# An attention-plus-MLP block on one core: a start for 512 tokens at a time, feature-major queries with block-ones sums, key normalisers moved to v, Mish in one instruction, both output products in one accumulation

## The chip, the core and the metric

The kernel runs on one core of one Trainium2 chip. A core has a tensor engine (PE), a vector engine (DVE), a scalar engine (ACT), GpSimd (POOL) and DMA queues. The metric is the device time of one execution in microseconds (us). Matmul results land in PSUM, which a kernel divides into banks; the program writes a bank again only when the engine that reads it is done. The granted clock is the share of its full speed that the profile records for PE. A profile's span, from its first to its last instruction, is about 1.7 us shorter than the measured time of the same execution.

## The reference, cut to what matters

There are S = 2048 tokens of width D = 512, 32 heads of width 16, and a hidden layer of F = 1792. All tensors are bf16.

```python
xn = layernorm(x)
# branch A: linear attention whose feature map is two softmaxes over 16 features
q, k, v = split_heads(xn @ wqkv)
pq, pk  = q @ w_phi, k @ w_phi                            # per head, 16x16
phi_q = concat(softmax(pq), softmax(-pq))
phi_k = concat(softmax(pk), softmax(-pk))
kv, z = sum_s phi_k[s] v[s]^T, sum_s phi_k[s]
o     = (phi_q @ kv) / (phi_q @ z + 1e-6)
A     = merge_heads(o) @ wo
# branch B: MLP with Mish
h = xn @ w1 + b1
B = (h * tanh(softplus(h))) @ w2
return x + A + B
```

`kv` and `z` sum over all tokens, so no token's attention output can begin before the last group of keys is in. Everything else can be done for one group of 512 tokens after another.

## The kernel before

The head projections are folded into the weights once (`wqp`, `wkp`). Then there is a loop over four groups of 512 tokens, and a closing phase for the attention output. The parts that the argument touches are these:

```python
# start: loads on two queues, statistics of ALL tokens before the loop
nc.scalar.dma_start(wqk[:], ...)            # 1 MB; scalar issues the loads of w1, w2 and the bias too
...
nc.scalar.dma_start(b1b[:], b1_v[:, :])     # 1792 biases, one element per descriptor
...
st[0] = stage_front(0)
finish_ln_stats()                           # loads the other 12 token tiles, bn_stats, one Sqrt

# stage_front: k and q token-major (tokens on partitions), exponentials of both
e1 = exp(ppkq); e2 = exp(-ppkq)             # 128 x 1024: plane 0 is k, plane 1 is q

# stage_phi: sums of 16 neighbours, normalise k twice and q once, all on the vector engine
nc.vector.reduce_sum(ss1[:], e1...);  nc.vector.reduce_sum(ss2[:], e2...)
...                                         # reciprocals, then e1k*=r1, e2k*=rk2, e1q*=ratio
# stage_kq: 32 tensor transposes and 8 vector copies turn q feature-major
# stage_h: uu = exp(h + b)                  (14 tiles of 128x512)
# stage_lt: Mish in three passes over 128 x 7168
nc.scalar.activation(th[:], uu[:], ACT.Ln, bias=1.0)      # softplus
nc.scalar.activation(uu[:], uu[:], ACT.Ln)                # h again
nc.scalar.activation(th[:], th[:], ACT.Tanh)
# stage_mb: act = lnu * th on vector (14 tiles), poB = act @ w2, copied to xb_all

for g in range(NG):
    uu = stage_h(st[g])
    if g > 0:
        stage_mb(st[g - 1], lt[g - 1])      # the PREVIOUS group's output product fills the passes
    lt[g] = stage_lt(uu)
    stage_phi(st[g]); stage_kq(st[g])
    if g + 1 < NG:
        st[g + 1] = stage_front(g + 1)
... kvm = kvacc * mask;  stage_mb(last)
# closing phase, per 512 tokens: attention products, normalise o, transpose,
# poA = ident @ x + oT @ wo, y = poA + xb_all
```

One property of the closing dependence helps later: the softmax of q needs no normaliser of its own. A common factor of both softmax planes cancels in `num / den`, so only the ratio of the two sums matters. The kernel before uses that (`ratio`).

The softmax here doesn't subtract the row's maximum and nothing guards it: scores larger than these inputs give would overflow.

Of the kernel before, what the change touches and what calls it, by code (L numbers as in the profile page):

```python
# [8 lines left out]
BF16 = mybir.dt.bfloat16  # L9
FP32 = mybir.dt.float32  # L10
# [7 lines left out]
def kernel(  # L18
# [12 lines left out]
    nc = tc.nc  # L31
# [6 lines left out]
    FT = F // P  # L38

    x2 = A_x.flatten_outer_dims()  # L40
    x_g = x2.rearrange("(g t p) d -> g p t d", t=TPG, p=P)
    o2 = out.flatten_outer_dims()
    out_g = o2.rearrange("(g t p) d -> g p t d", t=TPG, p=P)
# [5 lines left out]
    b1_v = B_b1.rearrange("(f p) -> p f", p=P)  # L49
# [5 lines left out]
    ident = consts.tile([P, P], BF16, name="ident")  # L55
    make_identity(nc, ident[:])

    U16f = consts.tile([8, P], FP32, name="U16f")
    nc.gpsimd.memset(U16f[:], 1.0)
    nc.gpsimd.affine_select(  # L60
        out=U16f[:],
        in_=U16f[:],
        pattern=[[1, P]],
        compare_op=ALU.is_ge,
        fill=0.0,
        base=0,
        channel_multiplier=-16,
    )
    nc.gpsimd.affine_select(
        out=U16f[:],  # L70
        in_=U16f[:],
        pattern=[[-1, P]],
        compare_op=ALU.is_ge,
        fill=0.0,
        base=15,
        channel_multiplier=16,
    )
    eps_t = consts.tile([P, 1], FP32, name="eps_t")
    nc.gpsimd.memset(eps_t[:], 1e-5)

    prep_w = tc.alloc_tile_pool(name="prep_w", bufs=1)
    xs_v = x2.rearrange("(g t p) d -> p (g t) d", t=TPG, p=P)
    x_stats0 = prep_w.tile([P, TPG, D], BF16, name="x_stats0")
    nc.sync.dma_start(x_stats0[:], xs_v[:, 0:TPG, :])
    wqk = prep_w.tile([P, KT, 2 * D], BF16, name="wqk")
    nc.scalar.dma_start(wqk[:], wqkv_v[:, :, 0 : 2 * D])
# [4 lines left out]
    nc.sync.dma_start(wv[:], wqkv_v[:, :, 2 * D : 3 * D])  # L91
    w1_sb = wts.tile([P, KT, F], BF16, name="w1_sb")
    nc.scalar.dma_start(w1_sb[:], w1_v[:, :, :])
    wo_sb = wts.tile([P, KT, D], BF16, name="wo_sb")
    nc.sync.dma_start(wo_sb[:], wo_v[:, :, :])
    w2_sb = wts.tile([P, FT, D], BF16, name="w2_sb")
    nc.scalar.dma_start(w2_sb[:], w2_v[:, :, :])
    b1b = wts.tile([P, FT], BF16, name="b1b")
    with nc.allow_non_contiguous_dma(reason="tiny bias load"):
        nc.scalar.dma_start(b1b[:], b1_v[:, :])  # L100
    b1f = wts.tile([P, FT], FP32, name="b1f")
    nc.vector.tensor_copy(b1f[:], b1b[:])

    phiqT_all = persist.tile([P, 8, S], BF16, name="phiqT_all")
    kvacc = persist.tile([P, 8, 136], FP32, name="kvacc")
    kvm = persist.tile([P, 8, 136], BF16, name="kvm")
    xb_all = persist.tile([P, NT, D], BF16, name="xb_all")
    mv = persist.tile([P, NT, nc.vector.BN_AGGR_DIM], FP32, name="mv")
    rstd = persist.tile([P, NT], FP32, name="rstd")

    stats0 = prep_w.tile([P, TPG, nc.vector.BN_STATS_DIM], FP32, name="stats0")
    for tt in range(TPG):
        nc.vector.bn_stats(stats0[:, tt, :], x_stats0[:, tt, :])
    for tt in range(TPG):
        nc.vector.bn_aggr(mv[:, tt, :], stats0[:, tt, :])
    nc.scalar.activation(rstd[:, 0:TPG], mv[:, 0:TPG, 1], ACT.Sqrt, bias=eps_t[:])
    nc.vector.reciprocal(rstd[:, 0:TPG], rstd[:, 0:TPG])

    def finish_ln_stats():
        statpool = tc.alloc_tile_pool(name="statpool", bufs=1)  # L120
        x_stats = statpool.tile([P, NT - TPG, D], BF16, name="x_stats")
        nc.sync.dma_start(x_stats[:], xs_v[:, TPG:NT, :])
        stats = statpool.tile([P, NT, nc.vector.BN_STATS_DIM], FP32, name="stats")
        for tt in range(TPG, NT):
            nc.vector.bn_stats(stats[:, tt, :], x_stats[:, tt - TPG, :])  # L125
        for tt in range(TPG, NT):
            nc.vector.bn_aggr(mv[:, tt, :], stats[:, tt, :])
        nc.scalar.activation(rstd[:, TPG:NT], mv[:, TPG:NT, 1], ACT.Sqrt, bias=eps_t[:])
        nc.vector.reciprocal(rstd[:, TPG:NT], rstd[:, TPG:NT])
        statpool.release()  # L130

    KVmask = consts.tile([P, 136], FP32, name="KVmask")
    B16b = consts.tile([P, P], BF16, name="B16b")
    Wbd = prep_w.tile([P, 4, P], BF16, name="Wbd")
# [3 lines left out]
    with ExitStack() as pctx:  # L138
        ps_prep = pctx.enter_context(
            tc.tile_pool(name="ps_prep", bufs=2, space=bass.MemoryType.PSUM)  # L140
        )
        ps_fold = pctx.enter_context(
            tc.tile_pool(name="ps_fold", bufs=4, space=bass.MemoryType.PSUM)
        )
        tmp = pctx.enter_context(tc.tile_pool(name="prep_tmp", bufs=2))

        pB = ps_prep.tile([P, P], FP32, name="pB", tag="prep")
        nc.tensor.matmul(pB[:], lhsT=U16f[:], rhs=U16f[:], start=True, stop=True)
        nc.vector.tensor_copy(B16b[:], pB[:])
        nc.vector.tensor_copy(KVmask[:, 0:P], pB[:])  # L150
        nc.vector.tensor_copy(KVmask[:, P : P + 8], pB[:, 0:P:16])

        nc.vector.tensor_tensor(
            out=Wbd[:].rearrange("p j (i e) -> p j i e", e=DH),
            in0=B16b[:, None, :]
            .rearrange("p o (i e) -> p o i e", e=DH)
            .to_broadcast([P, 4, 8, DH]),
            in1=Wsrc[:, :, None, :].to_broadcast([P, 4, 8, DH]),
            op=ALU.mult,
        )  # L160

        for mi, base_col in ((0, 0), (1, D)):
            pfs = [
                ps_fold.tile([P, D], FP32, name=f"pfold{mi}_{kt}", tag="fold")
                for kt in range(KT)
            ]
            for j in range(4):
                ptr = ps_prep.tile([P, D], BF16, name="ptrw", tag="prep")
                for kt in range(KT):
                    nc.tensor.transpose(  # L170
                        ptr[:, kt * P : (kt + 1) * P],
                        wqk[:, kt, base_col + j * P : base_col + (j + 1) * P],
                        ident[:],
                    )
                wT = tmp.tile([P, D], BF16, name="wT")
                nc.scalar.copy(wT[:], ptr[:])
                for kt in range(KT):
                    nc.tensor.matmul(
                        pfs[kt][:, j * P : (j + 1) * P],
                        lhsT=wT[:, kt * P : (kt + 1) * P],  # L180
                        rhs=Wbd[:, j, :],
                        start=True,
                        stop=True,
                    )
            dst = wqp if mi == 0 else wkp
            for kt in range(KT):
                nc.vector.tensor_copy(dst[:, kt, :], pfs[kt][:])
    prep_w.release()

    with ExitStack() as p1:  # L190
        xpool = p1.enter_context(tc.tile_pool(name="pa_x", bufs=1))
        xnpool = p1.enter_context(tc.tile_pool(name="pa_xn", bufs=1))
        xnTpool = p1.enter_context(tc.tile_pool(name="pa_xnT", bufs=2))
        spool = p1.enter_context(tc.tile_pool(name="pa_small", bufs=4))
        epool = p1.enter_context(tc.tile_pool(name="pa_e", bufs=4))
        vpool = p1.enter_context(tc.tile_pool(name="pa_v", bufs=2))
        mpool = p1.enter_context(tc.tile_pool(name="pa_mish", bufs=1))
        apool = p1.enter_context(tc.tile_pool(name="pa_act", bufs=14))
        ps_tr = p1.enter_context(tc.tile_pool(name="ps_tr", bufs=1, space=bass.MemoryType.PSUM))
        ps_kq = p1.enter_context(tc.tile_pool(name="ps_kq", bufs=1, space=bass.MemoryType.PSUM))  # L200
        ps_mm = p1.enter_context(tc.tile_pool(name="ps_mm", bufs=2, space=bass.MemoryType.PSUM))
        ps_kv = p1.enter_context(tc.tile_pool(name="ps_kv", bufs=1, space=bass.MemoryType.PSUM))
        ps_oB = p1.enter_context(tc.tile_pool(name="ps_oB", bufs=2, space=bass.MemoryType.PSUM))

        def stage_front(g):
            xg = xpool.tile([P, TPG, D], BF16, name="xg")
            nc.sync.dma_start(xg[:], x_g[g])
            xn = xnpool.tile([P, TPG, D], BF16, name="xn")
            for t in range(TPG):
                tt = g * TPG + t  # L210
                nc.vector.tensor_scalar(
                    out=xn[:, t, :],
                    in0=xg[:, t, :],
# [193 lines left out]
        for g in range(NG):  # L407
            uu = stage_h(st[g])
            if g > 0:
                stage_mb(st[g - 1], lt[g - 1])  # L410
# [120 lines left out]
```

## Time and profile before

| | us |
|---|---|
| time, median of 3 runs | 282.98 (282.32 to 284.24) |
| span of the profiled run | 281.6 |
| PE busy | 215.3 (76%), so idle 66.3 |
| vector busy | 198.0 (70%) |
| scalar busy | 167.0 (59%) |
| first dense projection matmul (a single one runs at 43.58) | 45.06 |

The first lines are from the page of the kernel before. They give busy time by engine (busy us, share of the span, number of instructions), then the span in 40 slices of 7 us, with each digit the busy tenths of a slice.

```profile
PE 215.3 (76%) x1277; PEld 108.9 (39%) x1298; DVE 198.0 (70%) x504; ACT 167.0 (59%) x136; POOL 2.1 (1%) x14
...
PE   1122238898783699986999996899997589889973
...
ACT  0040110777999587899787899868799900320330
```

No engine is full. PE has six slices of 1 to 3 at the left, dips to between 3 and 6 in the middle (about one per group), and a soft right end. The next view gives busy us per stage: the stretch and its length, then busy us and instruction count of each engine, the granted clock, and the DMA share and rate. The stretches are the start, the four groups, the last hidden output, and the attention output.

```profile
0.00:45.00 45.00, 11.70 (x80) 8.44 (x82) 19.05 (x53) 5.95 (x11) 1.64 (x12) 1.00 0.62 197
45.00:94.00 49.00, 38.10 (x218) 18.64 (x219) 35.71 (x73) 39.93 (x30) 0.20 (x1) 0.97 0.07 23
...
133.00:178.00 45.00, 41.48 (x239) 20.39 (x241) 36.76 (x78) 39.42 (x28) 0.00 (x0) 1.00 0.00 1
...
240.00:282.00 42.00, 32.33 (x240) 16.80 (x243) 28.57 (x128) 8.72 (x16) 0.00 (x0) 0.97 0.23 76
```

The start costs PE 33 us of idleness, and the last stretch 10. What PE waited for is named by the table of waits of the kernel before (waiting instruction, its releaser, us in all, times, longest):

```profile
PE pfold_0_185 L178 <- DVE wqp L187: 10.7, 1, 10.7
PE pfold_0_133 L178 <- ACT wT L176: 8.3, 2, 8.0
PE ptr L325 <- DVE phiqT_all L330: 8.2, 26, 0.7
PE poB L392 <- DVE act L384: 7.1, 2, 6.3
PE ptrw L170 <- DMA wqk<-in_A_wqkv_dram: 5.4, 1, 5.4
```

Three of these (10.7, 8.3 and 5.4) belong to the start. The scalar engine's copies (`wT`) come late because it issues loads first; the bias load alone took 8.14 us to issue, until 16.5. The chain of waits shows the rest. It holds a load of 21.78 us, then ten statistics instructions; the small weight copy that PE needed (`wqp`) stands behind them in the vector engine's order.

```profile
2.38 21.78 DMA x_stats<-in_A_x_dram
24.18 6.03 DVE stats L125 x10
...
32.94 2.34 DVE wqp L187 x4
```

The 8.2 us in 26 pieces is an alternation of transposes and vector copies. The 7.1 us is the Mish: the timeline of the scalar engine in group 0 (start, duration, instruction) shows a table load, two passes, another table load and a third pass, in which PE at last runs dry.

```profile
71.89 1.28 ACT L373 ACT_TABLE_LOAD   x1
73.19 6.18 ACT L373 ACTIVATE th<-uu 128x7168 bf16<-128x7168 bf16 x1
79.40 6.18 ACT L374 ACTIVATE uu<-uu 128x7168 bf16<-128x7168 bf16 x1
85.59 1.28 ACT L375 ACT_TABLE_LOAD   x1
86.89 6.18 ACT L375 ACTIVATE th<-th 128x7168 bf16<-128x7168 bf16 x1
```

### The profile page before, as it was taken

Reading aid. Unit: us, or ns where it says so; the run is one execution under the profiler, and the core shown is the slowest. Engines: PE = TensorE matmul, PEld = TensorE weight load, DVE = VectorE, ACT = ScalarE, POOL = GpSimd, SP = SyncE. Lnnn points to the kernel's source line nnn. Section 1 sums busy time; section 2 is a strip of 40 time slices with the busy share of each in tenths; the row PEclk is TensorE's granted clock in tenths of the full one; section 3 lists DMA queues with packets and bytes.
Section 4 is the critical chain, followed back from the end, with each engine's and each line's share of the span. In section 5 each row is a group of like instructions: output and inputs, shape, how many; then the busy total and the mean of one; then the engine's idle time right before and its main releaser. Section 6 shows DMA issues by size and latency. Waiting matters only on the chain.

```text
span 281.6 us, 3341 instructions
## 1 busy us (share of the span) xinstructions
PE 215.3 (76%) x1277; PEld 108.9 (39%) x1298; DVE 198.0 (70%) x504; ACT 167.0 (59%) x136; POOL 2.1 (1%) x14
## 2 busy tenths in 40 slices
PE   1122238898783699986999996899997589889973
PEld 0122214343541244445444445444444434444531
DVE  0405955999761799736899947699965783788762
ACT  0040110777999587899787899868799900320330
POOL 2000000000000000000000000000000000000000
PEclk9999999999999599999999999999999989999998
DMA  7996022200002000000000000000000300043022
GB/s 221 369 356 175 0 74 78 74 0 0 2 0 74 0 1 2 1 0 2 0 0 0 2 0 0 2 0 1 2 0 0 129 22 0 0 152 121 30 74 74
DMA packets 14687, 14.38 MB, mean 51 GB/s; under 512 B 2640, under 2 KB 13648, under 8 KB 14672
## 3 DMA queue, kind: packets, MB, share of 16 engines
q1 hardware_dynamic: 7360, 7.34, 8.0%
q10 hardware_dynamic: 7312, 6.84, 7.6%
q8 instruction: 10, 0.16, 0.2%
q14 instruction: 5, 0.04, 0.1%
HBM read 12.08 MB, written 2.10 MB: 50 GB/s over the span
## 4 chain that ended last, share of the span: by engine, by line
PE 52%; ACT 18%; DVE 13%; DMA 8%; issue 7%; SPq 1%; ACTq 0%; DVEq 0%
PE poB L392 13%; PE pmm L359 13%; DMA x_stats<-in_A_x_dram 8%; PE ppkq L249 5%; PE ppkq L257 5%; PE poA L490 5%; ACT th L373 4%; ACT th L375 4%; PE pmm L237 4%; DVE stats L125 3%; DVE o_t L458 2%; DVE phiqT_all L330 2%; PE ptr L325 2%; PE ptr L223 2%; DVE yg L497 1%
## 5 line engine op out<-in xcount | busy, mean ns | idle before, releaser
L392 PE MATMUL poB<-w_sb,act 128*128 128x512 bf16 x218 | 51.8, 387 | 7.3 <-DVE act L384 7.1
L359 PE MATMUL pmm<-xnT,w_sb 128*128 128x512 bf16 x219 | 52.1, 378 | 1.1 <-ACT uu L366 0.8
L366 ACT ACTIVATE uu<-pmm,b1f 128x512 bf16<-128x512 f32 x56 | 37.2, 691 | 11.8 <-PE pmm L359 7.6
L392 PEld LDWEIGHTS <-act 128*128 128x128 bf16 x224 | 22.2, 99 | 34.9 <-DVE act L384 9.3
L359 PEld LDWEIGHTS <-w_sb 128*128 128x128 bf16 x224 | 21.8, 97 | 28.9 <-issue 4.7
L400 DVE CAST xb_all<-poB 128x512 bf16<-128x512 f32 x16 | 11.1, 691 | 20.8 <-PE poB L392 20.8
L384 DVE TENSOR_TENSOR act<-uu,th 128x512 bf16<-128x512 bf16 x56 | 19.6, 416 | 7.9 <-ACT th L375 7.9
L374 ACT ACTIVATE uu<-uu 128x7168 bf16<-128x7168 bf16 x4 | 24.7, 6177 | 0.1
L373 ACT ACTIVATE th<-uu 128x7168 bf16<-128x7168 bf16 x4 | 24.7, 6177 | 0.0
L375 ACT ACTIVATE th<-th 128x7168 bf16<-128x7168 bf16 x4 | 24.7, 6177 | 0.0
L237 PE MATMUL pmm<-wv,xnT 128*128 128x512 bf16 x64 | 20.1, 395 | 0.2
L249 PE MATMUL ppkq<-wkp,xnT 128*128 128x512 bf16 x58 | 17.9, 400 | 1.2 <-ACT e_349 L267 0.5
L330 DVE COPY phiqT_all<-ptr 128x512 bf16<-128x512 bf16 x32 | 13.6, 424 | 7.1 <-PE ptr L325 7.0
L257 PE MATMUL ppkq<-wqp,xnT 128*128 128x512 bf16 x64 | 17.3, 394 | 0.0
L497 DVE TENSOR_TENSOR yg<-poA,xb_all 128x512 bf16<-128x512 f32 x16 | 10.7, 689 | 8.9 <-PE poA L490 8.7
L449 PE MATMUL pnd<-kvm,phiqT_all 128*128 128x136 bf16 x128 | 14.1, 228 | 3.6 <-DVE kvm L416 1.9
L125 DVE BATCH_NORM_STATS2 stats<-x_stats 128x6 f32<-128x512 bf16 x12 | 7.3, 676 | 13.6 <-DMA x_stats<-in_A_x_dram 13.6
L458 DVE TENSOR_TENSOR o_t<-pnd,rdt 128x128 bf16<-128x128 f32 x64 | 15.9, 286 | 0.1
L490 PE MATMUL poA<-wo_sb,oT 128*128 128x512 bf16 x60 | 15.7, 379 | 0.1
L223 PE MATMUL ptr<-ident,xn 128*128 128x128 bf16 x64 | 7.6, 238 | 7.5 <-issue 4.0
L228 DVE COPY xnT<-ptr 128x512 bf16<-128x512 bf16 x16 | 6.8, 425 | 8.5 <-PE ptr L223 8.5
L449 PEld LDWEIGHTS <-phiqT_all 128*128 128x128 bf16 x128 | 8.3, 98 | 10.9 <-DVE o_t L458 6.5
(386 smaller groups left out, 352.3 us busy)
## 6 DMA issues: line engine op xcount, KB each, us to landing
w_sb<-in_B_w_dram ACTq DMA_DIRECT2D x2, 1792.0 KB, 18.8
xg<-in_A_x_dram SPq DMA_DIRECT2D x4, 512.0 KB, 3.4
out_dram<-yg SPq DMA_DIRECT2D x4, 512.0 KB, 3.2
x_stats<-in_A_x_dram SPq DMA_DIRECT2D x1, 1536.0 KB, 21.8
wqk<-in_A_wqkv_dram ACTq DMA_DIRECT2D x1, 1024.0 KB, 7.5
x_stats_78<-in_A_x_dram SPq DMA_DIRECT2D x1, 512.0 KB, 6.1
wv<-in_A_wqkv_dram SPq DMA_DIRECT2D x1, 512.0 KB, 8.2
wo_sb<-in_A_wo_dram SPq DMA_DIRECT2D x1, 512.0 KB, 12.2
```

The source lines that it names most:

```text
L237: nc.tensor.matmul(pv[:], lhsT=xnT[:, kt, tok0 : tok0 + P], rhs=wv[:, kt, :], start=(kt == 0), stop=(kt == KT - 1),)
L249: nc.tensor.matmul(ppkq[:, 0, :], lhsT=xnT[:, kt, tok0 : tok0 + P], rhs=wkp[:, kt, :], start=(kt == 0), stop=(kt == KT - 1),)
L257: nc.tensor.matmul(ppkq[:, 1, :], lhsT=xnT[:, kt, tok0 : tok0 + P], rhs=wqp[:, kt, :], start=(kt == 0), stop=(kt == KT - 1),)
L359: nc.tensor.matmul(ph[:], lhsT=w1_sb[:, kt, f * P : (f + 1) * P], rhs=xnT[:, kt, :], start=(kt == 0), stop=(kt == KT - 1),)
L366: nc.scalar.activation(uu[:, f, :], ph[:], ACT.Exp, bias=b1f[:, f : f + 1])
L373: nc.scalar.activation(th[:], uu[:], ACT.Ln, bias=1.0)
L374: nc.scalar.activation(uu[:], uu[:], ACT.Ln)
L375: nc.scalar.activation(th[:], th[:], ACT.Tanh)
L392: nc.tensor.matmul(poB[:], lhsT=acts[f][:, t * P : (t + 1) * P], rhs=w2_sb[:, f, :], start=(f == 0), stop=(f == FT - 1),)
L449: nc.tensor.matmul(pnd[:], lhsT=phiqT_all[:, s, tok0 : tok0 + P], rhs=kvm[:, s, :], start=(pl == 0), stop=(pl == 1),)
L458: nc.vector.tensor_tensor(out=o_t[:, j * P : (j + 1) * P].rearrange("p (h e) -> p h e", e=16), in0=pnd[:, 0:128].rearrange("p (h e) -> p h ...
L490: nc.tensor.matmul(poA[:], lhsT=oT[:, j, t * P : (t + 1) * P], rhs=wo_sb[:, j, :], start=False, stop=(j == 3),)
```

## The change

The intent is to take work from the vector and scalar engines, so that PE runs without stalls. The core of the diff, with cuts (`...`), and comments added for the reader:

```diff
 # start: 512 tokens first, statistics per group, weights on the sync queue, bias as rows
-    nc.scalar.dma_start(wqk[:], wqkv_v[:, :, 0 : 2 * D])
+    for t in range(TPG):
+        nc.sync.dma_start(xgs[0][:, t, :], x_t[t])
+    nc.scalar.dma_start(wk_raw[:], wqkv_v[:, :, D : 2 * D])
...
-    b1_v = B_b1.rearrange("(f p) -> p f", p=P)
+    b1_v = B_b1.rearrange("(f p) -> f p", p=P)          # then one transpose
...
-        finish_ln_stats()
+    xnTs[0] = stage_ln(0)                # stage_ln(g + 1) later, inside the loop, with its own Sqrt
+    fold(wk_raw, wkp)
...
 # keys: normalise v (16 columns + normaliser per head), not the exponentials
-                nc.vector.tensor_tensor(out=e1[:, 0, :]..., in1=r1[:, 0, :, None]..., op=ALU.mult)
-                nc.vector.tensor_tensor(out=e2[:, 0, :]..., in1=rk2[:, :, None]..., op=ALU.mult)
+            nc.vector.tensor_tensor(out=v12[:, :, :, 0:DH], in0=pv..., in1=rk..., op=ALU.mult)
+            nc.gpsimd.tensor_copy(v12[:, :, :, DH], rk[:])
...
 # queries: made feature-major by the matmul itself; the sums of 16 by a block-ones matmul
-                    nc.tensor.transpose(ptr[...], planes[pl][t][:, 1, j * P : (j + 1) * P], ident[:])
-                nc.vector.tensor_copy(phiqT_all[:, s, gs], ptr[:])
+                        pq[:, jj, :], lhsT=wqp[:, kt, j * P : (j + 1) * P], rhs=xnT[:, kt, :],
+                    nc.tensor.matmul(pS[:], lhsT=B16b[:], rhs=eq[:, 1 - pl, jj, :], ...)
+                    nc.vector.tensor_tensor(out=eqT[:, pl * 4 + j, gs],
+                                            in0=pS[:], in1=eq[:, pl, jj, :], op=ALU.mult)
...
 # Mish: one instruction per 128x512 tile; `chain` keeps scalar work in program order
-            nc.scalar.activation(th[:], uu[:], ACT.Ln, bias=1.0)
-            nc.scalar.activation(uu[:], uu[:], ACT.Ln)
-            nc.scalar.activation(th[:], th[:], ACT.Tanh)
+                chain(nc.scalar.activation(act[:, f, :], ph[:, ff, :], ACT.Mish, bias=b1f[...]))
...
 # outputs: act @ w2 and oT @ wo in one PSUM accumulation, after the attention output; x added by vector
-                nc.vector.tensor_copy(xb_all[:, tt, :], poB[:])
-                nc.tensor.matmul(poA[:], lhsT=ident[:], rhs=xg2[:, t, :], start=True, stop=False)
+            for f in range(FT): nc.tensor.matmul(po[:], lhsT=act[:, f, ts], rhs=w2_sb[:, f, :], ...)
+            for j in range(4):  nc.tensor.matmul(po[:], lhsT=oT[:, j, ts], rhs=wo_sb[:, j, :], ...)
+            nc.vector.tensor_tensor(out=y[:], in0=po[:], in1=xg2[:, t, :], op=ALU.add)
```

The query trick: each plane is multiplied by the *sum of the other plane*. Plane 0 becomes e+ · S-, plane 1 e- · S+. Both differ from the two softmaxes by the common factor S+ · S-, which cancels in the division. No reciprocal is needed.

The order of the new kernel is: LayerNorm of group 0, fold of wk, then per group keys and v, (in group 0 only: fold of wq,) queries, LayerNorm of the next group, kv sums, hidden layer. In the program all output products stand behind the last kv sum, and the hidden layer of group 3 behind the first group's output. The scheduler moves a part forward: the first `act @ w2` matmuls run inside group 3.

## The prediction

> **What bounds the kernel now.** The busy table gives the tensor engine 76% of 281.6 us, vector 70%, scalar 59%; none is full throughout. The forty slices, the chain of waits and a table of busy time by stretch name four costs:
> - Start: until 44 us the tensor engine is busy only 11 us. The chain waits 21.8 us for the x_stats load, then 8 us of statistics, because vector work for the first tokens queues behind it; scalar is held until 16.6 us by issuing loads (one tiny bias load takes 8.1 us to issue).
> - Mish in three passes of 128x7168, 6.18 us each, plus two table loads of 1.28 us, per group. In 72-94, 125-133, 166-178 and 204-226 us the tensor engine is busy 60-75%, waiting for these or for alternating transposes and vector copies.
> - Groups: about 29-33 us each of dense tensor work, matmul starts 0.216 us apart.
> - The last 41 us: the attention output alone, small vector instructions (64 of 286 ns, 64 of 178 ns) between tensor pieces.
>
> **What the change does.**
> - Scalar: Mish is one activation per 128x512 tile. The Trainium skill ("ScalarE: Activation LUTs", step-by-step section) says the element rate doesn't depend on the function, so I cost it as the Exp of the same shape, 691 ns: 56 as before, and 74 us of three-pass work disappear. Added: xn and oT copies of 128x1024, about 0.95 us (estimate from 583 ns for 512), and three table loads of 1.28 us per group. Total about 167 -> 110 us.
> - Vector: 198 -> about 125 us. Per group about 21 us: four reductions (1.21 us), four reciprocals (0.54), four v products of 1024 elements (about 1.2), eight eqT products (0.69), LayerNorm 4, kv sums 1.4.
> - Tensor: 128 transposes of phi_q and 16 identity matmuls go, 32 block-ones matmuls come; 736 instead of 720 matmuls of 512 columns. At 0.216 us for these and 0.056-0.058 us for the 128/136-column ones the stream costs about 180 us unstalled. Tensor work is NOT reduced much; the gain is in stalls.
> - The output product now accumulates in one bank and fills the tensor engine while the attention output is normalised, so the final 41 us stretch becomes dense.
>
> **Sum.** First k matmul at about 16 us (was 45). Group 0: q's folded weight copies stand behind the v products in vector order, so the tensor engine stalls some 10 us before q; group ends at about 57. Groups 1 and 2: 27 us of tensor work, with 2-3 us lost to vector/scalar handoffs (sums, table loads), 29 each: 115. Group 3, without its hidden layer but with output filler: 25, 140. Remaining 260 output matmuls (56 us), last hidden layer (12), attention products and transposes (11), stalls 3: 222. Tail 3-4 us.
>
> Predicted 225 us, likely 211 to 240 (ratio about 0.80). Chances: faster by over 2% 0.97; within 2% 0.02; slower 0.01.
>
> **What would show it.** First dense tensor work before 20 us; Mish groups of 56 at about 0.69 us; table loads about 14 at 1.28 us; tensor busy share above 85% after 60 us; vector about 125 us, scalar about 110 us; a tensor hole of about 10 us before q of group 0, released by vector; the last 80 us nearly without tensor gaps.
>
> **What would make it wrong.** The block-ones product and the eqT product ping-pong through two PSUM banks shared with transposes and kv sums, so in-order tensor instructions may wait longer on vector than I allow (+5 us a group). GpSimd copies of the normalisers could hold up the kv product. Loads could land late at the start. A faster stream might be granted a lower tensor clock (it is 0.978 now). On the other side, the group 0 hole could be smaller.

## The result, and the profile after

| | before | after |
|---|---|---|
| time, median | 283.61 of 4 runs (282.32 to 284.73) | 232.65 of 4 runs (230.99 to 233.77) |
| span of the profiled run | 281.6 | 229.3 |
| PE busy / idle | 215.3 / 66.3 | 197.9 / 31.4 |
| vector busy | 198.0 | 120.2 |
| scalar busy | 167.0 | 101.3 |
| mean granted clock | 0.978 | 0.978 |

The ratio is 0.8192 (95% interval 0.8143 to 0.8241). A ratio here is the mean time of one kernel's fast runs over the mean of the other's fast runs of the same rounds, so it isn't quite the ratio of the medians quoted. The mean granted clock is that of the profiled runs; the other runs of the kernel after had 0.978 and, the two slower ones, 0.963.

The span fell by 52.3 us: 34.9 of idle and 17.4 of busy PE time (the trace before lacks 21 of its 1298 matmul records, so the split is good to a few us). Here are the lines of the page after that answer to those shown before (a slice is now 5.7 us):

```profile
PE 197.9 (86%) x1185; PEld 99.1 (43%) x1185; DVE 120.2 (52%) x205; ACT 101.3 (44%) x124; POOL 8.5 (4%) x26
...
PE   0089168889999999999999599899999999999993
...
ACT  0266500995889677896778400142663002000300
...
L365 ACT ACTIVATE act<-ph,b1f 128x512 bf16<-128x512 f32 x56 | 35.2, 686 | 22.9 <-PE ph L355 15.7
```

The left edge has shrunk from 42 us to 11, and behind it there is a new hole (the 1 and 6 after 89). One 5 remains at about 129 us. The rest is dense. The last line is the Mish group (count, then busy us, mean ns of one, idle before): 56 instructions of 686 ns. Busy time by stage of the kernel after shows the same; the stretches are the time until the first k matmul, two halves of group 0, group 1, (group 2 is alike,) group 3 until its kv sums, and the output in two parts.

```profile
0.00:18.40 18.40, 6.10 (x62) 4.88 (x63) 6.86 (x19) 5.43 (x6) 1.57 (x10) 1.00 0.93 302
18.40:36.00 17.60, 9.74 (x51) 4.39 (x48) 15.27 (x24) 6.98 (x7) 1.73 (x4) 0.90 0.33 104
36.00:60.20 24.20, 22.62 (x136) 11.43 (x134) 15.15 (x35) 16.05 (x21) 0.00 (x0) 0.93 0.07 23
60.20:88.90 28.70, 27.83 (x162) 13.68 (x161) 18.83 (x28) 22.38 (x28) 1.74 (x4) 1.00 0.07 19
...
117.50:141.00 23.50, 20.29 (x108) 9.52 (x106) 16.60 (x22) 10.20 (x11) 1.74 (x4) 0.93 0.00 1
141.00:182.00 41.00, 39.80 (x253) 20.00 (x251) 14.12 (x26) 14.00 (x19) 0.00 (x0) 1.00 0.09 30
182.00:229.00 47.00, 43.77 (x270) 21.61 (x267) 14.56 (x26) 3.85 (x4) 0.00 (x0) 1.00 0.13 43
```

Groups 1 and 2 take 28.7 us each and PE works in 27.8 of them. Group 0 takes 41.8 us (18.35 to 60.16) for about the same work and the fold of wq. The table of waits of the kernel after names its holes: the 11.3 us is the load and LayerNorm of the first tokens, and the vector engine's v products (`v_260`, `v_296`, `v_308`) hold PE three times.

```profile
PE ptr L191 <- DVE xn L176: 11.3, 1, 11.3
PE pv L258 <- DVE v_260 L274: 4.8, 1, 4.8
PE po L418 <- DVE v_1202 L274: 2.9, 1, 2.9
PE pf L228 <- DVE v_296 L274: 2.1, 1, 2.1
```

Their place is seen in the timeline of PE (in brackets, the idle time before and what ended it): the second token pair's v matmuls behind a hole of 4.79 us, then another hole, then the fold of wq (`pf`) in pieces, then the first q matmul at 36.03 us.

```profile
28.71 3.22 PE L258 MATMUL pv<-wv,xnT 128*128 128x512 bf16 x8 [4.79 <-DVE v_260 L274]
34.05 0.38 PE L228 MATMUL pf<-Wbd,wT 128*128 128x128 bf16 x4 [2.11 <-DVE v_296 L274]
...
36.03 1.06 PE L319 MATMUL pq<-xnT,wqp 128*128 128x512 bf16 x2
```

PE doesn't pass the waiting instructions here: the hidden-layer matmuls, whose weights and tokens were on the chip (no load ran from 24 to 36 us), begin only at 42.88. The folded weights share two PSUM banks with the v products and are copied out by the vector engine, so the fold that q needs waits until the v products of four token tiles are done, and these wait for the sums over the key exponentials. Behind the holes PE also ran at a lower granted clock: 0.76 from 28.7 to 36 us and 0.58 from 36 to 40.

### The profile page after: what moved, and what is told of

It is laid out like the page before. It is cut to its first block, busy times and chain, and to the rows that moved or that the text cites. A ratio compares the mean times of both kernels' runs of the same rounds, so it can differ in the third digit from the quotient of the medians.

```text
span 229.3 us, 2898 instructions
## 1 busy us (share of the span) xinstructions
PE 197.9 (86%) x1185; PEld 99.1 (43%) x1185; DVE 120.2 (52%) x205; ACT 101.3 (44%) x124; POOL 8.5 (4%) x26
## 4 chain that ended last, share of the span: by engine, by line
PE 61%; ACT 18%; DVE 12%; issue 4%; DMA 3%; SPq 1%; ACTq 0%
PE po L418 21%; PE ph L355 17%; PE po L426 6%; DVE ss L266 5%; PE pkv L294 3%; ACT act L365 3%; PE pq L319 3%; PE pnd L380 3%; DMA xg<-in_A_x_dram 3%; ACT L251 2%; ACT L171 2%; PE ptr L191 2%; ACT ek L252 2%; ACT ek L251 2%; ACT eq L327 2%
## 5 line engine op out<-in xcount | busy, mean ns | idle before, releaser
L418 PE MATMUL po<-w_sb,act 128*128 128x512 bf16 x224 | 56.0, 386 | 2.9 <-DVE v_1202 L274 2.9
L355 PE MATMUL ph<-xnT,w_sb 128*128 128x512 bf16 x224 | 54.7, 379 | 1.7 <-ACT act L365 1.7
L365 ACT ACTIVATE act<-ph,b1f 128x512 bf16<-128x512 f32 x56 | 35.2, 686 | 22.9 <-PE ph L355 15.7
L266 DVE TENSOR_REDUCE ss<-ek 128x64 f32<-128x1024 bf16 x16 | 18.7, 1212 | 24.2 <-ACT ek L252 24.2
L340 DVE TENSOR_TENSOR eqT<-pS,eq 128x512 bf16<-128x512 f32 x32 | 20.5, 687 | 4.1 <-PE pS L333 4.1
L258 PE MATMUL pv<-wv,xnT 128*128 128x512 bf16 x64 | 16.9, 404 | 4.8 <-DVE v_260 L274 4.8
L319 PE MATMUL pq<-xnT,wqp 128*128 128x512 bf16 x64 | 16.6, 405 | 0.9 <-ACT ek L252 0.9
L426 PE MATMUL po<-wo_sb,oT 128*128 128x512 bf16 x64 | 16.9, 380 | 0.0
L191 PE MATMUL ptr<-ident,xn 128*128 128x128 bf16 x64 | 6.1, 242 | 11.3 <-DVE xn L176 11.3
L243 PE MATMUL pk<-wkp,xnT 128*128 128x512 bf16 x64 | 15.4, 379 | 0.0
L333 PE MATMUL pS<-eq,B16b 128*128 128x512 bf16 x32 | 11.5, 378 | 0.9 <-ACT eq L328 0.9
L389 DVE RECIPROCAL rd<-pnd 128x32 f32<-128x32 f32 x16 | 5.6, 349 | 11.5 <-PE pnd L380 11.5
```

The costliest lines, as they stand in the source:

```text
L243: nc.tensor.matmul(pk[:, tt, :], lhsT=xnT[:, kt, tok0 : tok0 + P], rhs=wkp[:, kt, :], start=(kt == 0), stop=(kt == KT - 1),)
L258: nc.tensor.matmul(pv[:], lhsT=xnT[:, kt, tok0 : tok0 + P], rhs=wv[:, kt, :], start=(kt == 0), stop=(kt == KT - 1),)
L266: nc.vector.reduce_sum(ss[:], ek[:, :, tt, :].rearrange("p s (h e) -> p s h e", e=DH), axis=AX.X,)
L319: nc.tensor.matmul(pq[:, jj, :], lhsT=wqp[:, kt, j * P : (j + 1) * P], rhs=xnT[:, kt, :], start=(kt == 0), stop=(kt == KT - 1),)
L333: nc.tensor.matmul(pS[:], lhsT=B16b[:], rhs=eq[:, 1 - pl, jj, :], start=True, stop=True,)
L340: nc.vector.tensor_tensor(out=eqT[:, pl * 4 + j, gs], in0=pS[:], in1=eq[:, pl, jj, :], op=ALU.mult,)
```

## The experiments

Twelve kernels were run. All gave correct results. The runs of the kernel before on the same chip had medians of 283.42 (e1 to e4), 283.78 (e5 to e8) and 283.62 us (e9 to e12); the ratios are to those. Differences between experiments are differences of medians, in part from different chips; the medians of the kernel before differ by 0.4 us. The diffs below are abridged, and some lines put in words what the code does. "The fold-first kernel" is the kernel of e4.

### e1: the kernel before with one-pass Mish alone

```diff
-                nc.scalar.activation(uu[:, f, :], ph[:], ACT.Exp, bias=b1f[:, f : f + 1])
+                chain(nc.scalar.activation(act[:, f, :], ph[:], ACT.Mish, bias=b1f[:, f : f + 1]))
-            th = Ln(uu + 1); uu = Ln(uu); th = Tanh(th)      # three passes; 14 vector products go too
```

> The kernel before with one activation per hidden tile in place of three passes and the vector product, scalar instructions kept in program order; nothing else changed. Theory A (Mish passes hold the old main loop): the tensor holes of 8.8 us in 72-94 us and of about 3 us in each later round of transposes close, and the output products fill the transposes: about 262 us (-20). Theory B (the old main loop hides the passes behind dense tensor work except in the first group, and the start is the larger part of the gain): only the first hole goes, about 274 us (-9).

Measured: 264.75 us, ratio 0.9338 (0.9300 to 0.9376), so 18.7 us less. Scalar fell from 167.0 to 94.0 us and vector from 198.0 to 178.4. Ninety-three us of busy time on two engines went, and the time fell by a fifth of that. Theory A was nearly right in size. The rest had been hidden: while the passes run, the timeline of the kernel before has PE at the previous group's output product (115.4 to 124.2 us beside the passes from 117.6), at transposes and kv sums, and at the next group's projections.

### e2 and e5: the kernel before with the start changed alone

```diff
 # e2: weights from the sync queue, bias as rows, and statistics per group inside stage_front
-        nc.scalar.dma_start(w1_sb..), (w2_sb..), (b1b..)
+        nc.sync.dma_start(w1_sb..), (w2_sb..);  nc.scalar.dma_start(b1row[:], b1_v)
-        finish_ln_stats()
+            if g > 0: bn_stats(..); bn_aggr(..); rstd[:, gt] = Sqrt(..); reciprocal(..)
 # e5: the same loads, but the statistics of all tokens stay together, with x_stats second in its queue
```

> The kernel before with only its start repaired: statistics of groups 1 to 3 computed from the group's own load when it comes, hidden and output weights issued from the sync engine instead of scalar, bias loaded as rows and transposed. Theory B: first dense matmul at about 25 us instead of 45 us, nearly all kept: about 263 us (-20). Theory A: the earlier start is given back in the first Mish wait, -8 us or less.

> The kernel before with the loads re-ordered alone: the x_stats load second in its queue instead of behind two weights, hidden and output weights issued by the sync engine, bias as rows. No Sqrt is added inside the loop, which had split the Mish passes in the earlier run of the start (273.1 us). Theory: first dense matmul at about 28 us instead of 45 us, all kept: 266 us (-17). Rival: an earlier start meets the same Mish wait and is given back in part there: 273 us or more.

e2 measured 273.09 us (0.9637, 0.9601 to 0.9673), 10.3 less, although its first dense matmul came 16.7 us earlier (28.35 instead of 45.06), so 6.4 us were given back. This lies between the theories, nearer to A. The scalar timeline shows a reason for the difference: the added Sqrt of each group falls between the Mish passes and brings table loads (Ln at 57.03, Sqrt's table at 63.23, Ln's table again at 64.84, Tanh's at 72.32). e11 tests it.

e5 measured 276.80 us (0.9745, 0.9710 to 0.9781). The expectation was missed, because the edit did not do what it was for: the first projection matmul came at 37.23 us (43.58 before), not near 28. The 12 statistics now stood before the small `KVmask` copies in the vector order, and the fold waited 11.16 us for them. The 6.4 us that its start gained were kept (the time fell by 7.0).

### e3: the kernel after with Mish in three passes

```diff
+        th = thpool.tile([P, FT, 512], BF16, name="th")
-                        act[:, f, :], ph[:, ff, :], ACT.Mish, bias=...
+                        act[:, f, :], ph[:, ff, :], ACT.Exp, bias=...
+        th = Ln(act + 1); act = Ln(act); th = Tanh(th)            # chained in order
+        for f in range(FT): act[:, f] *= th[:, f]                 # on vector
 # two pools smaller so that th fits: ek 4 -> 3, v12 6 -> 4
```

> The changed kernel with Mish again as Exp, two Ln and a Tanh of 128x7168 (6.18 us each) and 14 vector products; two pools made smaller to make room, not expected to matter. Theory A: in the new order nothing hides them; groups 0 to 2 become scalar bound, about +14 us each, 273 us (262 to 285). Theory B: hidden by output filler, below 245 us.

Measured: 312.29 us (1.1026, 1.0967 to 1.1085), 79.6 us more than the kernel after and slower than the kernel before. No theory expected that much. Its tables of waits, for PE and then for the vector engine, show where it goes:

```profile
PE pq L320 <- ACT ek L253: 57.5, 3, 19.2
...
DVE act L375 <- ACT th L373: 79.5, 4, 26.4
```

Three times, once per group, the next group's exponentials stand behind the passes in the scalar order, and PE waits 19 us for them with nothing else to do; the fourth passes end in a late output. PE is busy 210.8 of 312.5 us and its granted clock falls to 0.85. The kernel before could hide the passes behind the previous group's output product. The kernel after has moved all output products to the end, and so has nothing to hide them with. So one-pass Mish was worth 18.7 us in the kernel before, and the change as arranged can't do without it. "The share of Mish in the gain" has no single value. That the missing filler is the reason is read from the waits and not tested alone: this kernel also keeps all scalar instructions in program order by `chain`, which the kernel before doesn't, and two pools are smaller.

### e4: the kernel after with the fold of wq right after the fold of wk

```diff
     fold(wk_raw, wkp)
+    fold(wq_raw, wqp)
...
         if g == 0:
-            fold(wq_raw, wqp)
             prep_w.release()
```

> The changed kernel with q's weight fold placed before the first k and v products instead of after them, so its vector copies no longer stand behind the four v products. Theory: the 10 us tensor hole between 24 and 36 us is due to that order; most of it goes, about 224 us (-8). Rival: the hole is due to vector sums for v themselves, which hold the tensor engine through the two v banks; then it only moves, and less than 3 us is won.

Measured: 220.03 us (0.7752, 0.7713 to 0.7792), 12.6 us less than the kernel after. The PE timeline of this kernel at the same place:

```profile
23.83 1.89 PE L258 MATMUL pv<-wv,xnT 128*128 128x512 bf16 x8
25.55 3.62 PE L319 MATMUL pq<-xnT,wqp 128*128 128x512 bf16 x15
```

The hole is gone, q starts at 25.55 instead of 36.03, and group 1's keys at 48.64 instead of 60.16. Group 0 takes 30.0 instead of 41.8 us: 8.4 us less idle, and 3.4 us that the kernel after lost there at the lower clock (1.00 throughout in e4). So the hole cost more than its idle time. The theory had the cause, and expected 8 us. All later stages keep the distance to within 0.3 us. This two-line move, which adds and removes no instruction, is worth as much as the larger parts of the change below.

### e6: fold-first, with the key normalisers back on the exponentials

```diff
-            v12 = vpool.tile([P, 2, NH, VW], BF16, name="v12");  v12 = pv * rk   (two planes)
-            nc.gpsimd.tensor_copy(v12[:, :, :, DH], rk[:])
+            v12 = vpool.tile([P, NH, VW], BF16, name="v12");     v12 = copy(pv); column DH = 1
+            ek *= rk                                             # 128 x 1024 on vector
```

> The fold-first kernel (220.0 us) with the key normalisers multiplied onto the exponentials again and v copied with a column of ones. Theory: vector gains about 2.4 us a group but has slack, and the v banks are free at once, so the 2.9 us hole before group 3's output filler goes: 218 us (216 to 221). Rival: vector is what holds the group, and normalisers on v are worth 2 us a group: 226 us or more.

Measured: 231.57 us of 6 runs (0.8141, 0.8102 to 0.8180), 11.5 us more than e4. The theory that the vector engine, busy 55% of the span in e4, would absorb 10 us more (it had 129.9 instead of 120.1) fell. The profiled run was the fastest of the six (229.00), so its trace shows 9.3 us of the difference. Seven of them are lost in group 0, whose vector engine had no slack: in e4 it is busy in 29.96 of the 31 us from 18 to 49. A part of the seven is again the clock, 0.89 in this stretch and 1.00 in e4. The others come in groups 1 and 2, at 1.4 us each (30.1 instead of 28.7). The table of waits of this kernel:

```profile
PE pS L335 <- DVE eqT L342: 5.0, 5, 3.5
PE ph L357 <- ACT act L367: 4.0, 2, 2.0
```

The first line is for the most part group 0: PE stands before the block-ones sums (`pS`), since the vector engine is late in freeing their banks. The second is groups 1 and 2: the scheduler moved the v matmuls ahead of the table switch, so that nothing is left to fill it (2.0 us instead of 0.5). So the effect has a part that is vector work and a part that is a different order of the PE stream.

### e7: fold-first, with token-major queries

```diff
-                        pq[:, jj, :], lhsT=wqp[:, kt, j * P : (j + 1) * P], rhs=xnT[:, kt, :],
+                        pq[:, tt, :], lhsT=xnT[:, kt, tok0 : tok0 + P], rhs=wqp[:, kt, :],
-                    pS = B16b @ eq(other plane);  eqT = pS * eq
+                sq = reduce_sum(eq);  rq = 1/sq0;  ratio = sq1 * rq;  eq0 *= ratio     # vector
+                32 transposes and 8 copies into eqT per group
```

> The fold-first kernel with queries token-major again: sums by vector reductions, ratio product, 32 transposes and 8 copies of 128x512 a group instead of 8 block-ones products and 8 products out of PSUM. Theory: vector rises from about 19 to 26 us a group of 29, tensor work about equal; the last transposes find no filler: 229 us (+9, range 225 to 236). Rival: no more than 2 us, since the tensor engine is the limit.

Measured: 234.11 us (0.8240, 0.8208 to 0.8271), 14.1 us more than e4, within the expected range. Vector rose to 144.0 us. A group takes 31.4 us instead of 28.7, and the alternation of transposes and copies, which the kernel before has too (8.2 us there), is back: PE waits 4.1 us in 13 pieces for the copies.

### e8: fold-first, with the two output products apart

```diff
+        if g > 0: stage_mb(g - 1, acts[g - 1])      # act @ w2 inside the loop, copied to xb_all
-            po = act @ w2 + oT @ wo;            y = po + x
+            po = ident @ x + oT @ wo;           y = po + xb_all[tt]
 # the hidden layer of group 3 moves from the output phase into the loop; act buffers 3 -> 2
```

> The fold-first kernel with the two output products in banks of their own again: the hidden one copied to SBUF inside the loop, x added by an identity matmul, the sum on vector. Theory: the last stretch has only attention work again and waits on vector between the pieces: 230 us (+10, range 226 to 236), tensor idle in the last 35 us about 8 us. Rival: the filler was not needed, +4 us for the 16 identity matmuls alone.

Measured: 219.69 us (0.7757, 0.7724 to 0.7790), the same as e4. The expected loss of 10 us did not come. Busy time by stretch of this kernel, two stretches (the loop's end, then the attention output):

```profile
130.00:180.00 50.00, 49.37 (x252) 23.48 (x255) 23.75 (x33) 17.78 (x23) 1.73 (x4) 1.00 0.00 1
180.00:218.00 38.00, 30.12 (x266) 18.22 (x267) 26.48 (x49) 7.71 (x8) 0.00 (x0) 0.98 0.25 84
```

The attention output alone leaves PE idle 7.9 of 38 us, and that includes the tail after the last matmul; in e4 it is 3.8 in the same stretch. But the output products inside the loop fill what e4 leaves idle there: the hole of 2.9 us in group 3 is gone, and from 130 to 180 us PE is idle 0.6 us, in e4 1.7. With the hole goes e4's loss of clock behind it (see e10): the mean clock of e8's runs was 0.998 to 1.000, of e4's 0.989 to 0.997. The sixteen identity matmuls and sixteen copies come on top. It sums to nothing. The hidden layer of group 3 came into the loop with this edit, and its part was not separated.

### e9: an attempt to start earlier still

```diff
-    nc.scalar.dma_start(wq_raw[:], ...)           # behind wk_raw
+    nc.sync.dma_start(wq_raw[:], ...)             # ahead of wv
+    nc.scalar.activation(warm[:], eps_t[:], ACT.Sqrt)    # dummy, loads the Sqrt table early
-    xnTs[0] = stage_ln(0); fold(wk_raw, wkp); fold(wq_raw, wqp)
+    wkT = fold_t(wk_raw)                          # transposes and copies of wk first
+    xnTs[0] = stage_ln(0); fold_m(wkT, wkp); fold_m(fold_t(wq_raw), wqp)
```

> The fold-first kernel (220.0 us, first k matmul at about 18.5 us) with the raw query weights on the other load queue ahead of wv, a dummy Sqrt that loads its table before the statistics are ready, and the transposes and copies of wk ahead of the LayerNorm of group 0. Theory (the start is on the critical path in full because vector and tensor are both dense from there on): first k matmul at 14 to 15.5 us, time 3 to 4.5 us shorter, 215.5 to 217. Rival (group 0 is vector-bound, 29.96 busy us of 31, so an earlier first k matmul only lengthens the waits for the vector engine's folds and v products): group 1 starts within 1.5 us of 48.6 as before, time 218.5 to 220.5.

Measured: 223.94 us (0.7891, 0.7866 to 0.7916), slower than e4 by 3.9 us. The first k matmul came at 13.99, 4.6 us earlier, as the theory had it, and group 1 began at 53.25, 4.6 us *later*. Both expectations were off; the rival had the mechanism, but it expected nothing lost. The PE timeline of this kernel:

```profile
18.83 0.38 PE L233 MATMUL pf<-Wbd,wT 128*128 128x128 bf16 x4 [1.85 <-DVE wqp L240]
...
33.22 0.38 PE L338 MATMUL pS<-eq,B16b 128*128 128x512 bf16 x1 [1.35 <-DVE eqT L345]
...
39.95 2.00 PE L193 MATMUL ptr<-ident,xn 128*128 128x128 bf16 x16 [3.33 <-DVE xn L178]
```

In e4's stream the six late sums `pS` alternate with hidden-layer matmuls, and cost nothing. Here the hidden-layer matmuls stand ahead of them, the six sums come one after another, each waiting for the vector engine, and then PE waits 3.3 us for the LayerNorm of group 1, which has come later in the vector order. From group 1 to the end the two kernels take the same (169.5 and 169.4 us). So an earlier start of PE didn't shorten group 0, and the new order of instructions made it longer: from 18 to 53 us the vector engine is busy 27.8 of 35 us here, no longer full, and PE's clock is 0.95. Three edits were made at once; e10 tries one of them alone.

### e10: fold-first, with the dummy Sqrt alone

```diff
+    warm = consts.tile([P, 1], FP32, name="warm")
+    nc.scalar.activation(warm[:], eps_t[:], ACT.Sqrt)
```

> The fold-first kernel with the dummy Sqrt alone. The table load of 1.28 us stands between the statistics and rstd only if it isn't loaded already while the x load is awaited. Theory: it moves off the path, 1.3 us, so 218.7. Rival: the statistics are not the last thing that the first k matmul waits for (the folded wk is), so 220.0 plus or minus 0.3.

Measured: 218.85 us (0.7706, 0.7677 to 0.7735), the fastest of all by its median. Its interval overlaps that of e4, and the traces warn against reading the two profiles' spans (215.8 and 218.0) as the effect: the first k matmul and group 1 come only 0.5 us earlier. The other 1.7 us is the clock, as group 1 to the end takes 169.4 us in e4 and 167.7 in e10. Both kernels have the same hole of 2.9 us in group 3. Directly after it the two look like this, first e4 and then e10, in busy time by stretch (the 1.00 or 0.62 near the end is the granted clock):

```profile
120.00:122.00 2.00, 1.56 (x4) 0.55 (x4) 2.00 (x3) 0.00 (x0) 0.00 (x0) 0.62 0.00 0
122.00:124.00 2.00, 2.00 (x6) 0.76 (x5) 0.71 (x2) 0.00 (x0) 0.00 (x0) 0.52 0.00 0
```

```profile
119.50:122.00 2.50, 2.07 (x10) 0.97 (x10) 2.50 (x4) 0.00 (x0) 0.00 (x0) 1.00 0.00 0
122.00:124.00 2.00, 2.00 (x11) 0.88 (x9) 1.91 (x4) 0.00 (x0) 0.00 (x0) 1.00 0.00 0
```

For 3.4 us (120.5 to 123.9) e4's PE ran at half speed (nine output matmuls took 3.79 us, in e10 2.10), and e10's did not. The Trainium skill ("TensorE: Matmul & The Clock Gate", section "What's actually happening") describes a clock that is either full or half, decided by how busy PE was in a window of about 3.4 us that runs free of the program. Our reading, which the page doesn't state, is that a hole a little shorter than the window may then trip it in one execution and not in another. This pair agrees with that, and the half-speed stretch is as long as the window; in the kernel after, the same hole is followed by one of 3.4 us too (mean clock 0.66 from 131 to 136). More than this it can't show. Runs of equal mean clock can be compared as well: at 0.992 the spans are 218.0 and 216.9, at 0.997 they are 216.6 and 215.8, at 0.989 they are 218.6 or 218.7 and 217.5. (A mean clock also counts stretches that cost nothing: all that e10's profile lost lies after its last matmul.) So the table load off the start is worth 0.5 us by the marks in the traces and 0.8 to 1.1 by the spans, against 1.3 expected. A part of the rest is hidden: the first transposes begin 0.9 us earlier, and then the fold of wq waits 0.7 us for the vector engine's copy of the folded wk.

### e11: the kernel before with e1 and e2 together

```diff
 # the edits of e1 and e2; the Sqrt of each group is in the chained order too
+                chain(nc.scalar.activation(rstd[:, gt], mv[:, gt, 1], ACT.Sqrt, bias=eps_t[:]))
```

> The kernel before with both partial changes: one-pass Mish in chained order (18.7 us alone) and per-group statistics with re-ordered loads (10.3 us alone, although its first dense matmul moved 16.7 us). Theory A (the per-group Sqrt ate 6 us of the start by falling between the three Mish passes; without those passes it cannot): first dense matmul at 28, gains 33 to 35 us, 248.5 to 250.5. Theory B (the gains simply add): 29 us, 254.4. Theory C (they overlap, since a later phase sets the pace): 258 or more.

Measured: 251.52 us (0.8878, 0.8837 to 0.8919), 32.1 us less than before, and 31.8 by its ratio, against 29.1 if the two gains of 18.8 and 10.3 (one minus each ratio, times 283.62) only added. The first projection matmul came at 26.46 (43.58 before, 26.86 in e2). With the three passes gone, the start keeps 13.0 us of the 17.1 by which it comes earlier, in e2 10.3 of 16.7. So what is given back fell from 6.4 to 4.1 us, and the table loads between the passes can have eaten 2 to 3 us, not the 6 of theory A, which missed its range by 1 us. The distance from plain addition is 2.7 us, and the intervals of the three ratios (1.1 us each way, so about 2 together) leave little of it sure. Of the 4.1 us still given back, the trace names longer waits for Mish (5.1 us, 1.9 in e1); the waits for the exponentials are as in e1 (2.6 and 2.5). This was not taken apart further.

### e12: the kernel before with one-pass Mish, scalar order left to the scheduler

```diff
 # e1 without the chain
-                chain(nc.scalar.activation(e1[:], ppkq[:], ACT.Exp))
+                nc.scalar.activation(e1[:], ppkq[:], ACT.Exp)
```

> The kernel before with one-pass Mish but without the dependency that keeps scalar instructions in program order, so that Exp and Mish alternate and about 14 more pairs of table loads appear (28 at 1.28 us, 36 us of scalar work on top of 94). Theory (the order is needed: a table load stands inside the loop from hidden matmul to activation to the release of its PSUM buffer, so part of it is exposed): 278 to 295, the gain of one-pass Mish is lost. Rival (scalar was busy only 36% and absorbs it): 265 to 269.

Measured: 265.82 us (0.9371, 0.9333 to 0.9410), 1.1 us more than e1, which the intervals (1.1 us each way) don't tell from nothing. The rival was right. The scalar timeline of this kernel shows the tables changing for every two tiles:

```profile
60.91 1.28 ACT L265 ACT_TABLE_LOAD   x1
62.20 1.02 ACT L265 ACTIVATE e<-ppkq 128x1024 bf16<-128x1024 f32 x1
63.12 1.02 ACT L266 ACTIVATE e<-ppkq 128x1024 bf16<-128x1024 f32 x1
64.16 1.28 ACT L365 ACT_TABLE_LOAD   x1
65.45 1.26 ACT L365 ACTIVATE act<-pmm,b1f 128x512 bf16<-128x512 f32 x2
```

Twenty-four more loads of 1.283 us raised scalar's busy time from 94.0 to 123.9 us, and PE's wait for Mish rose only from 1.9 to 6.6 us. In this kernel the ordered form is worth almost nothing in time. Its runs also had a lower clock (0.947 to 0.981) than these (0.985 to 0.994); in the profiles the difference lies in the first group (0.84 and 0.96 from 43 to 75 us). What the extra loads cost at equal clock was not measured. In the kernel after, where the same dependency is used, it was not tried.

## Why the prediction was right, point by point

The prediction said 225 us (211 to 240); it was 232.65 us.

- **Mish and the scalar engine: right.** 56 instructions of 686 ns (said 691), scalar 101.3 us (said 110), 12 table loads (said 14). The cost was taken from the Trainium skill ("ScalarE: Activation LUTs", "Step-by-step: what each stage is for"), which says that the element rate doesn't depend on the function; the trace agrees within 1%.
- **Vector: right.** 120.2 us against 125. The smaller load mattered more than the average suggests: e6 and e7 put 10 and 24 us back and lost 11.5 and 14.1 us.
- **The stages: right but for the first.** Groups 28.7 us (said 29); the last kv sums at 141 us (said 140), the last output matmul at 225.8 (said 222). The first k matmul came at 18.35, not 16, and group 0 ended at 60.2, not 57. The groups lost 0.9 us each to handoffs, not 2 to 3, but had 27.8 us of tensor work, not 27. The last matmul was 3.8 us late, the tail (3.5) was as said, the time is 1.7 us longer than the span, which the prediction had not set apart, and the profiled run was the fastest of the four by 1.7 us against the median. These make up nearly all of the 7.6 us.
- **The hole in group 0: right.** It was said to be some 10 us, before q, released by the vector engine; it is 7.9 us of idle PE in four pieces. Another 3.4 us went with it at the lower clock, which the prediction didn't count. The prediction took the hole for given. Moving one line removed it and 12.6 us with it (e4), so the change as made keeps less of its earlier start than it could.
- **"Tensor work is NOT reduced much": half right.** PE busy fell by 17.4 us, a third of the gain. The issue rate as predicted (0.216 us per 512 columns) gives only about 4 us of that: 128 transposes at 0.057 and 16 identity matmuls go, and 32 block-ones matmuls come. The rest is most likely that a matmul which stands alone counts for its whole latency (379 ns for 512 columns, about 220 for 128), while in a dense stream the latencies overlap (eight matmuls of 512 columns take 1.89 us in the lines above). The profile models the ends of matmuls, so this was argued and not tested.
- **"The output product fills the tensor engine … so the final stretch becomes dense": true as seen, wrong as a reason.** The stretch is dense, but e8 does without the merged product and takes the same time. The same matmuls fill either the loop or the end. The prediction counted a filled hole as a gain without asking what that filler had been filling before.
- **The risks named** did not come: the block-ones sums waited 0.9 us in the whole trace, and that for scalar's exponentials; GpSimd's copies released no wait of weight, and the clock was 0.978 in the profiled run (0.963 in two others; the kernel before had 0.941 to 0.978). e6 and e9 show that the first of these was close, though: with a little more vector work, or another order, PE does stand before `pS`.

Of the 51 us, then, the start brings the first dense matmul forward by 26.7 us (45.06 to 18.35), of which the hole in group 0 gives 12 back, as e4 shows. In e11 one-pass Mish and a faster start give 32 us together. The feature-major queries and the v normalisers are worth 14 and 11.5 us, measured by undoing each in the fold-first kernel. The merged output is worth nothing there. The new start was tried only in the kernel before, and the rest of the edits (fewer and larger PSUM tiles, copies moved to scalar) not alone. These parts don't add up to one sum, and e3 shows why: what a part is worth depends on what the others leave to hide it.

The fastest kernel found is e10, at 218.85 us: the change, with the fold of wq moved up and a dummy Sqrt.

## What to carry to other kernels

Ask of every long pass on a side engine what PE does meanwhile, and of every filler what it was filling before: the same three-pass Mish cost 19 us with the previous group's output product to hide behind, and 80 without it (and with all scalar work chained in order). As PE didn't pass a waiting instruction here, look for a cheap copy (here four of about 0.65 us, of folded weights) that stands in another engine's queue behind work that isn't needed yet; moving it was worth 12.6 us. The busy share of an engine over the whole span says little about slack: the vector engine was at 55% and full in group 0.

## What the Trainium skill lacked or had wrong

- "ScalarE: Activation LUTs", section "What ACT_TABLE_LOAD costs", states about 1283 ns for a load and about 1380 ns of drain, 2.66 us for every switch. The load agrees (1283 ns in every run here), but no drain is seen around it: before the change, the load at 71.89 us begins as the previous activation ends, and the next one begins at 73.19, so a switch takes 1.30 us. Counted from start to start in e12, an activation behind a switch follows 2.33 us after the one before it (63.12 to 65.45), and 0.92 us without a switch, so the switch adds 1.41 us.
- The same page, section "Table sets: the hidden batching unit", has the rule to batch calls by table set. e12 broke it with 24 extra loads and paid 1.1 us in 265 (within the noise, and at a higher clock), since the scalar engine had the time. The page doesn't say when the rule matters.
- No page names Mish. Here it is one instruction of 686 ns for 128x512 with a bias, as fast as Exp (691), and a table load stands between it and Exp and between it and Sqrt.
